# Attention in pairs of units, the first mixture in blocks of 256 tokens, the logits four tiles at a time

## The chip, the core and the metric

The kernel runs on one core of one Trainium2 chip. The metric is device time in microseconds (us) of one launch, the median of three runs. The engines are named as the profile names them: PE (TensorE, matmuls), DVE (VectorE), ACT (ScalarE), POOL (GpSimd) and SP (SyncE, which issues the DMAs). Every engine works off its own list of instructions strictly in the order in which the program wrote them.

## The reference

Three stages follow each other, all in float32. Cut to what matters:

```python
for t in range(S):                                   # attention: (B,H,S,D) = (4,8,768,48)
    cur = einsum('bhd,bhe->bhde', u[None] * kt, vt)
    y[:, :, t] = einsum('bhd,bhde->bhe', rt, state + cur)
    state = wt[..., None] * state + einsum('bhd,bhe->bhde', kt, vt)
x = y as (3072, 384)
x = ((x @ w1) * (x @ w2)) @ w3 @ w_out               # first mixture, 384 -> 1024 -> 384
logits = x @ w_gate                                  # 8 experts, then 8 rounds of row and column norms
out = sum_e P[:, e:e+1] * (relu(x @ w1[e]) @ w2[e])  # second mixture, weighted by the normed P
```

## The kernel before

**Attention.** The 3072 tokens are 24 units of 128 tokens. In a unit the recurrence is written as small matmuls: `sc` (64x64 scores of the keys K and the receptances R), `trn` (four 128x128 transposes of K), `yt1` (scores times values), `up` (the state's increment), `Sn` (the new state, eight short DVE instructions) and `yt2` (R times the old state), 64x64 tiles in the corners of the PE. Before them DVE and POOL prepare a unit: two scans of the decay (`scan_f` L279, `scan_g` L283), `ks` and `rp` (products with k and r, L296 and L300), `kx`, `rx`, `rk` and `ec` on POOL (L306, L312, L274 and L275, L321), `cc` on DVE.

**First mixture.** The tokens go through in eight blocks of 384 (`BLK`). For each of eight slices f of the hidden width there are nine matmuls `pa` and nine `pb` (high and low parts of x and of the weights, two tiles of 128x384 per tag and so at most two `pb` on their way), ACT copies `pa` (`asb`), DVE multiplies it with `pb` (`gs`, L478), ACT and POOL split the product (`gh`, `gl`). Then 72 matmuls `po` with the folded weights give the x of the second mixture. That is 8*18 + 72 = 216 matmuls of 384 columns a block. `moe_log` (L528) forms a block's logits: nine small matmuls `pl`, a DVE copy, one transpose `plt`, a DVE copy.

**Second mixture.** For n = 0 to 63 (four batches of 768 tokens times sixteen pairs of hidden slices) the program runs `zp` matmuls of 256 columns and `yp` matmuls of 384. Sums and differences of x tiles that it needs are made ahead by `pre_x` (sums L699, low parts L706, then a DMA to memory); DVE does this for the first three batches during the attention.

**What sets the order.** Units 0 to 6 come from the hand-written list `START`, which the change leaves alone. From slice `S0 = 28` on, a loop over slices s does in each slice one f of `pa`/`pb`, or one of four parts of `po`, and one phase of unit n = s // 4: phase 1 is [`yt2` of the unit before, `sc`, `trn`], phase 2 is [`yt1`, `up`, `Sn`], and the last unit of a block has its `yt2` in phase 3. The preparation of the next unit waits in the queue `aux`, two entries a slice, and `pre_x` sits at places in a table (`PLACES`, `LASTPLACES`). Every attention input has two buffers (`nat[nm, u_ % 2]`). All matmuls are written by the helper `mm`, L114, so the trace shows one line for them.

Of the kernel before, what the change touches and what calls it, by code (L numbers as in the profile page):

```python
# [61 lines left out]
def tile_rwkv_moe_sinkhorn_moe(  # L62
# [28 lines left out]
    BLK = 384  # L91
    UB = BLK // P
    NB = NT // BLK
# [4 lines left out]
    T = 256  # L98
# [26 lines left out]
    lt = const.tile([GP * UB, P], F32, name="lt")  # L125
# [167 lines left out]
    def ks(n):  # L293
        st[n]["K"] = t = att.tile([P, 34 * 32], F32, tag="K", bufs=1, name="Kt")
        gv = st[n]["G"][:, 1:529].rearrange("p (c b s) -> p b c s", b=2, s=33)[:, :, :, 1:33]
        (nc.gpsimd if n in KS_POOL else nc.vector).tensor_tensor(diag(t), nat["k", n % 2].rearrange("p (a b s) -> p b a s", b=2, s=32), gv, op=ALU.mult)  # L296

    def rp(n):
        st[n]["R"] = t = att.tile([P, 34 * 32], F32, tag="R", bufs=2, name="Rt")
        (nc.gpsimd if n in RP_POOL else nc.vector).tensor_tensor(off(t)[:, ::-1], nat["r", n % 2].rearrange("p (a b s) -> p b a s", b=2, s=32),  # L300
                                tot(n)[:, :, :, 0:32], op=ALU.mult)

    def kx(n):
        t = st[n]["K"]
        for g, m_ in enumerate((st[n]["M"][:, 1, :], tot(n)[:, 1, :, 32])):
            nc.gpsimd.tensor_tensor(off(t)[:, g], diag(t)[:, 1 - g], m_.unsqueeze(2).to_broadcast([P, 8, 32]),  # L306
                                    op=ALU.mult)

    def rx(n):
        t = st[n]["R"]  # L310
        for g, m_ in enumerate((st[n]["M"][:, 0, :], tot(n)[:, 0, :, 32])):
            nc.gpsimd.tensor_tensor(diag(t)[:, g], off(t)[:, 1 - g], m_.unsqueeze(2).to_broadcast([P, 8, 32]),  # L312
                                    op=ALU.mult)
# [11 lines left out]
    def sc(n):  # L325
        Rt, Kt = st[n]["R"], st[n]["K"]
        st[n]["sc"] = s_ = [psa.tile([P, NP, DP], F32, tag=f"sc{h}", name=f"sc{h}") for h in range(2)]
        for p in range(NP):
            for c in range(2):
                for h in range(2):  # L330
                    cs = slice((4 * p + 2 * c) * 32, (4 * p + 2 * c + 2) * 32)
                    mm(s_[h][64 * c:64 * c + 64, p, :], Kt[64 * h:64 * h + 64, cs], Rt[64 * h:64 * h + 64, cs],
                       True, True, pos=(64 * h, 64 * c))

    def trn(n):
        if n - 1 in st:
# [4 lines left out]
        for p in range(NP):  # L341
            mm(pn[:, p, :], st[n]["K"][:, (16 + 4 * p) * 32:(20 + 4 * p) * 32], ident, True, True, tr=True)

    def kn_(n):
        st[n]["kn"] = t = att.tile([P, NP, P], F32, tag="kn", name="kn")
        nc.scalar.activation(t, st[n]["pn"], AF.Copy)
# [8 lines left out]
    def yt1(n):  # L355
        d = st[n]
        A, vt = d["A"], nat["v", n % 2].rearrange("p (h d) -> p h d", d=DP)
        d["yp"] = yp = [psa.tile([P, NP, DP], F32, tag=f"yt{c}", name=f"yt{c}") for c in range(2)]
        for p in range(NP):
            for h in range(2):  # L360
                for c in range(2):
                    rs = slice(64 * c, 64 * c + 64)
                    o = 64 * (h if c else 1 - h)
                    mm(yp[c][o:o + 64, p, :], vt[rs, 2 * p + h, :], A[rs, h, p, :],
                       p == 0, n % UPB == 0 and c == 0 and p == NP - 1, pos=(64 * c, o))

    def up_(n):
        d = st[n]
        vt = nat["v", n % 2].rearrange("p (h d) -> p h d", d=DP)
        d["up"] = up = [psa.tile([P, NP, DP], F32, tag=f"sc{c}", name=f"up{c}") for c in range(2)]  # L370
        for p in range(NP):
            for h in range(2):
                for c in range(2):
                    rs = slice(64 * c, 64 * c + 64)
                    mm(up[c][64 * h:64 * h + 64, p, :], d["kn"][rs, p, 64 * h:64 * h + 64], vt[rs, 2 * p + h, :],
                       True, True, pos=(64 * c, 64 * h))

    def sn_(n):
# [3 lines left out]
        for c in range(2):  # L382
            sn = att.tile([P, NP, DP], F32, tag="S", bufs=3, name="Sn")
# [12 lines left out]
    def yt2(n):  # L396
        yp, ss, Rt = st[n]["yp"], st[n]["ss"], st[n]["R"]
        for p in range(NP):
            for h in range(2):
                for c in (1, 0):  # L400
# [16 lines left out]

    def xd_(n):
        blk, q = n // UB, n % UB
        xt = xr[blk]  # L420
        if blk == NB - 1 or q == UB - 1:
            ts_ = slice(q * P, (q + 1) * P) if blk == NB - 1 else slice(0, BLK)
            for j in range(KD):
                for h in range(2):
                    nc.sync.dma_start(xt[64 * h + D:64 * h + 64, j, ts_],
                                      xt[64 * h + DQ * j:64 * h + DQ * (j + 1), NP - 1, ts_])

    def stage_a0(n):
        rk(n)
        aux.extend([lambda f=f: f(n) for f in (scan_f, scan_g, small, ks, rp, kx, rx)] + [lambda: (cc(n), ec(n))])  # L430

    def each(n, *fs):
        for f in fs:
            f(n)
# [3 lines left out]
    def x_high(blk, q=None):  # L438
        xt = xr[blk]
        if blk not in xs:  # L440
            xhl = moe.tile([P, 2, KD, BLK], F32R, tag="xhl", name="xhl")
            xs[blk] = (xhl[:, 0], xhl[:, 1])
        xh, xl = xs[blk]
        ts_ = slice(0, BLK) if q is None else slice(q * P, (q + 1) * P)
        nc.scalar.activation(xh[:, :, ts_], xt[:, 0:KD, ts_], AF.Copy)

    def x_low(blk, q=None):
        xt = xr[blk]
        xh, xl = xs[blk]
        ts_ = slice(0, BLK) if q is None else slice(q * P, (q + 1) * P)  # L450
        nc.vector.tensor_tensor(xl[:, :, ts_], xt[:, 0:KD, ts_], xh[:, :, ts_].bitcast(F32), op=ALU.subtract)
# [5 lines left out]
    def ab(blk, f, nm, wh, wl):  # L457
        xh, xl = xs[blk]
        m_t[nm, blk, f] = pt = ps.tile([P, BLK], F32, tag={"pa": "mA", "pb": "mB"}[nm], bufs=2, name=nm)
# [47 lines left out]
    def moe_x2(blk, i, parts=X2S):  # L507
        gh, gl = g_t[blk]
        n_ = KD * NF * 3 // parts
        for m in range(i * n_, (i + 1) * n_):  # L510
            q, rest = divmod(m, 3 * NF)
            f, c = divmod(rest, 3)
            if rest == 0:
                if 0 not in x2:
                    x2_open()
                po_t[blk] = ps.tile([P, BLK], F32, tag="mAmB"[2 * (q % 2):][:2], bufs=2, name="po")
# [3 lines left out]
            if rest == 3 * NF - 1:  # L520
                t0, t1 = blk * BLK, (blk + 1) * BLK
                while t0 < t1:
                    dst, o = x2_at(q, t0)
                    n = min(T - o, t1 - t0)
                    nc.scalar.activation(dst[:, o:o + n], po[:, t0 - blk * BLK:t0 - blk * BLK + n], AF.Copy)
                    t0 += n

    def moe_log(blk, step, pool=None, tag="mA", bufs=2):  # L528
        pool = pool or ps
        if step == 0:  # L530
            pl = pool.tile([GP * UB, P], F32, tag=tag, bufs=bufs, name="pl")
# [728 lines left out]
```

## Time and profile before

| | |
|---|---|
| median of 3 runs | 1915.16 us (1914.37 to 1915.44) |
| profiled execution | 1915.92 us, of which the span from the first to the last instruction is 1914.2 us |
| PE busy | 99% of the span |
| DVE, ACT, POOL busy | 72%, 36%, 34% |
| granted clock | 1.00 |

A busy share counts the time in which at least one instruction of the engine is on its way. The attention and the first mixture run together until about 437 us; after that the second mixture alone runs to the end.

### The profile page before, as it was taken

Reading aid. Unit: us, or ns where it says so; the run is one execution under the profiler, and the core shown is the slowest. Engines: PE = TensorE matmul, PEld = TensorE weight load, DVE = VectorE, ACT = ScalarE, POOL = GpSimd, SP = SyncE. Lnnn points to the kernel's source line nnn. Section 1 sums busy time; section 2 is a strip of 40 time slices with the busy share of each in tenths; the row PEclk is TensorE's granted clock in tenths of the full one; section 3 lists DMA queues with packets and bytes.
Section 4 is the critical chain, followed back from the end, with each engine's and each line's share of the span. In section 5 each row is a group of like instructions: output and inputs, shape, how many; then the busy total and the mean of one; then the engine's idle time right before and its main releaser. Section 6 shows DMA issues by size and latency. Waiting matters only on the chain.

```text
span 1914.2 us, 38103 instructions
## 1 busy us (share of the span) xinstructions
PE 1888.8 (99%) x15499; PEld 1842.9 (96%) x15499; DVE 1378.7 (72%) x2409; ACT 686.2 (36%) x1322; POOL 650.0 (34%) x867
## 2 busy tenths in 40 slices
PE   6999999999999999999999999999999999999999
PEld 3799999999999999999999999999999999999999
DVE  8866777765887887676767677667677777667666
ACT  6733333344333333333333333333333333333322
POOL 6766666635431313122222222222323231322200
PEclk9999999999999999999999999999999999999999
DMA  9622444346655555555555555555555555555463
GB/s 379 230 87 91 140 134 140 105 148 239 235 184 191 190 196 197 182 199 183 202 188 197 185 200 187 193 176 208 175 200 185 197 194 193 191 182 188 173 204 121
DMA packets 90494, 353.76 MB, mean 185 GB/s; under 512 B 10384, under 2 KB 34256, under 8 KB 64592
## 3 DMA queue, kind: packets, MB, share of 16 engines
q1 hardware_dynamic: 90320, 351.34, 53.1%
q8 instruction: 122, 2.00, 0.4%
q14 instruction: 52, 0.43, 0.1%
HBM read 329.67 MB, written 20.45 MB: 183 GB/s over the span
## 4 chain that ended last, share of the span: by engine, by line
PE 94%; DMA 2%; DVE 2%; ACT 1%; issue 0%; SPq 0%; DVEq 0%; ACTq 0%
PE yp L114 41%; PE zp L114 34%; PE po L114 5%; PE pa L114 5%; PE pb L114 5%; DMA raw<-in_moe_w_dram 1%; PE yt L114 1%; PE w34ps L114 1%; PE trn L114 1%; DMA nat_kn<-in_kn_dram 1%; PE sc L114 1%; PE up L114 0%; PE pl L114 0%; DVE cvp L229 0%; DVE Sn L388 0%
## 5 line engine op out<-in xcount | busy, mean ns | idle before, releaser
L114 PE MATMUL zp<-xc,w1c 128*128 128x256 f32 x5760 | 793.7, 277 | 1.0 <-DVE ct L915 0.6
L114 PEld LDWEIGHTS zp<-xc,w1c 128*128 128x128 f32 x5760 | 766.7, 188 | 4.8 <-ACT ct L922 1.3
L114 PE MATMUL yp<-w2h,hl 128*128 128x384 f32 x1536 | 515.0, 335 | 0.6 <-DVE hl L912 0.6
L114 PE MATMUL yp<-w2l,hh 128*128 128x384 f32 x1536 | 514.6, 335 | 0.0
L114 PE MATMUL yp<-w2h,hh 128*128 128x384 f32 x1536 | 513.1, 334 | 0.0
L907 ACT ACTIVATE hh<-ct 128x512 fp32r<-128x512 f32 x384 | 236.8, 632 | 526.3 <-DVE ct L915 265.8
L915 DVE TENSOR_TENSOR ct<-ct,zp 128x512 f32<-128x512 f32 x576 | 377.3, 681 | 47.0 <-PE zp L114 41.4
L620 POOL TENSOR_TENSOR w1c<-w1s,w1c 128x512 fp32r<-128x512 f32 (+1 forms) x120 | 127.6, 1064 | 779.9 <-ACT w1c L616 779.9
L922 ACT ACTIVATE ct<-zp 128x512 f32<-128x512 f32 x256 | 153.6, 600 | 440.8 <-PE zp L114 440.8
L114 PEld LDWEIGHTS yp<-w2h,hl 128*128 128x128 f32 x1536 | 288.3, 188 | 1.0 <-DVE hl L912 0.9
L114 PEld LDWEIGHTS yp<-w2h,hh 128*128 128x128 f32 x1536 | 288.4, 188 | 0.2 <-issue 0.2
L114 PEld LDWEIGHTS yp<-w2l,hh 128*128 128x128 f32 x1536 | 288.4, 188 | 0.0
L1087 DVE SCALAR_TENSOR_TENSOR acc<-yp,Pm,acc 128x384 f32<-128x384 f32 x336 | 205.8, 613 | 103.9 <-PE yp L114 103.8
L912 DVE SCALAR_TENSOR_TENSOR hl<-ct,hh 128x512 fp32r<-128x512 f32 x384 | 276.5, 734 | 0.0
L918 DVE TENSOR_TENSOR ct<-ct,zp 128x512 f32<-128x512 f32 x128 | 87.9, 687 | 162.8 <-PE zp L114 162.8
L918 DVE TENSOR_TENSOR ct<-zp,ct 128x512 f32<-128x512 f32 x128 | 88.3, 690 | 74.6 <-ACT ct L922 62.7
L620 POOL TENSOR_TENSOR w1c<-w1raw,w1c 128x128 fp32r<-128x128 f32 (+1 forms) x90 | 56.7, 630 | 195.3 <-ACT w1c L616 195.3
L612 POOL TENSOR_TENSOR w1s<-w1raw 128x128 f32<-128x128 f32 x240 | 120.8, 524 | 0.2
L487 POOL TENSOR_TENSOR gl<-gs,gh 128x384 fp32r<-128x384 f32 x64 | 75.4, 1179 | 104.0 <-ACT gh L483 101.2
L114 PE MATMUL pa<-xhl,w1h 128*128 128x384 f32 x384 | 100.4, 342 | 1.5 <-ACT w34s L255 1.5
L114 PE MATMUL pb<-xhl,w2h 128*128 128x384 f32 x384 | 98.1, 336 | 0.4 <-DVE cv L230 0.4
L478 DVE TENSOR_TENSOR gs<-pb,asb 128x384 f32<-128x384 f32 x64 | 35.4, 553 | 66.6 <-PE pb L114 48.1
(130 smaller groups left out, 1908.6 us busy)
## 6 DMA issues: line engine op xcount, KB each, us to landing
xc<-xd SPq DMA_DIRECT2D x192, 1024.0 KB, 4.9
xc<-xd SPq DMA_DIRECT2D x64, 768.0 KB, 4.3
xd<-x2s SPq DMA_DIRECT2D x53, 256.0 KB, 2.7
w1raw<-in_e_w_dram SPq DMA_DIRECT2D x32, 384.0 KB, 3.1
w2raw<-in_e_w_dram SPq DMA_DIRECT2D x32, 384.0 KB, 3.1
raw<-in_moe_w_dram SPq DMA_DIRECT2D x8, 1024.0 KB, 9.5
nat_w<-in_w_dram SPq DMA_DIRECT2D x24, 264.5 KB, 3.4
nat_k<-in_kt_dram SPq DMA_DIRECT2D x24, 256.0 KB, 4.0
```

Source lines behind the costliest of these rows:

```text
L114: nc.tensor.matmul(o, lhsT, rhs, start=start, stop=stop, **kw)
L478: nc.vector.tensor_tensor(t, m_t.pop(("pb", blk, f)), m_t.pop(("asb", blk, f)), op=ALU.mult)
L487: nc.gpsimd.tensor_tensor(gl[:, f, :], m_t.pop(("gs", blk, f)), gh[:, f, :].bitcast(F32), op=ALU.subtract)
L612: eng.tensor_tensor(tmp_[:, many.index(r), :], at_(a), at_(b), op=ALU.add if sg == 1 else ALU.subtract)
L620: eng.tensor_tensor(lo[:, d0:d1, :], sv, hi[:, d0:d1, :].bitcast(F32), op=ALU.subtract)
L907: nc.scalar.activation(hh, src, AF.Relu)
L912: nc.vector.scalar_tensor_tensor(hl, src, 0.0, hh.bitcast(F32), op0=ALU.max, op1=ALU.subtract)
L915: nc.vector.tensor_tensor(o, a, b_, op=ALU.add)
L918: nc.vector.tensor_tensor(o, a, b_, op=ALU.subtract)
L922: nc.scalar.activation(t, src, AF.Copy)
L1087: nc.vector.scalar_tensor_tensor(dst, yp, so["Pm"][:, tt, e:e + 1], dst, op0=ALU.mult, op1=ALU.add)
```

## The change

Units 0 to 6 stay as they are. The blocks of the first mixture are now 384, 384 and then nine of 256 tokens. From unit 7 on (unit 7 by itself, then 8 and 9, 10 and 11, up to 22 and 23) a block of 256 tokens goes with a pair of units, in a cycle c of 24 steps: eight steps of nine `po` matmuls, then sixteen that are alternately a `pa` and a `pb`. At the start of a cycle stands `turn`: `yt2` of both old units, `sc` of both new ones, `trn` of both. After step 8 stands `middle`: `yt1` of both, `up` of both, then `Sn` of both. The preparation of the two units of the next cycle (`prep`) is placed by steps.

K and R are now pairs of half tiles, so `ks` and `rp` are two DVE instructions each; they take over the second input buffers, and from unit 10 on the inputs r, k, w, rn and kn have one buffer each. The logits are formed in groups of four tiles of 128 tokens, six groups instead of eight blocks. All of the third batch's `pre_x` now comes before the second mixture starts, and three of the eight first weight preparations of the second mixture (`sp_w1`) go to POOL.

```diff
-    BLK = 384
+    T = 256
+    BLKS = [(0, 384), (384, 384)] + [(t, T) for t in range(768, NT, T)]
+    FU = 6
+    NC = NB - 2
+    def src(nm, u_):
+        return nat[nm, u_ % 2 if u_ < ONE or nm == "v" else 0]
...
-    def sc(n):
-        st[n]["sc"] = s_ = [psa.tile([P, NP, DP], F32, tag=f"sc{h}", name=f"sc{h}") for h in range(2)]
+    def pair(nm):
+        return [psa.tile([P, 2, NP, DP], F32, tag=f"{nm}{c}", name=f"{nm}{c}") for c in range(2)]
+
+    def sc(*us):
+        s_ = pair("sc")
...
-    def moe_log(blk, step, pool=None, tag="mA", bufs=2):
+    UL = P // GP
+    def moe_log(grp, step, pool=None, tag="mA", bufs=2):
...
+    def turn(k_old, k_new):
+        old, new = (units(k) if 0 <= k <= NC - 1 else () for k in (k_old, k_new))
+        for n in old:
+            yt2(n)
+        if new:
+            front(*new)
+        if old:
+            xraw(*old)
+            xd_(old[-1])
+        if new:
+            front_end(*new)
...
+    for k in range(NC):
+        step(k, -0.5, lambda k=k: turn(k, k + 1))
+        step(k, 4.6, lambda k=k: x_high(k + 2))
+        step(k, 5.6, lambda k=k: x_low(k + 2))
+        if k + 1 < NC:
+            step(k, 9 - 0.5, lambda k=k: middle(*units(k + 1)))
+        if k + 2 < NC:
+            n = FU + 2 * k + 4
+            prep(n, 24 * k + 1)
+            prep(n + 1, 24 * k + 12)
...
+            if sb_ < NS - 2:
+                t_, w_, d_ = 24 * 3 * sb_ + 9.7 + 4.2 * m_, WORK[m_ % 4], (5, 9)
...
+    for c in range(-1, NC):
+        for j in range(10 if c < 0 else 0, 24):
+            run(24 * c + j)
+            if j < 8:
+                moe_x2(c + 1, j, 8)
+            else:
+                f = (j - 8) // 2
+                if j % 2 == 0:
+                    pa(c + 2, f)
+                    asb(c + 2, f)
+                else:
+                    pb(c + 2, f)
+                    gs(c + 2, f)
```

What this does to the order, first on PE, at the place where unit 9 ends and unit 10 begins. Before (of the rows of `yt` and of `sc`, which alternate between two tiles, the first two stand):

```order
L114 MATMUL pb<-xhl,w2h 128x384 x2
L114 MATMUL pb<-xhl,w2l 128x384
L114 MATMUL yt_2479<-Rt,Sn 64x64
L114 MATMUL yt_2478<-Rt,Sn 64x64
...
L114 MATMUL sc_2648<-Rt,Kt 64x64
L114 MATMUL sc_2649<-Rt,Kt 64x64
...
L114 MATMUL trn<-ident,Kt 128x128 x4
L114 MATMUL pa<-xhl,w1h 128x384 x2
```

One unit's `yt2`, `sc` and `trn` stand between two runs of wide matmuls. The same place of PE in the changed kernel, where units 8 and 9 end and 10 and 11 begin (`nat_n`, `nat_k`, `nat_w`, `kn` and `s_more` are buffers that now hold halves of K and R, and states):

```order
L113 MATMUL pb<-xhl,w2l 128x256
L113 MATMUL yt_2193<-Rt,nat_n_109 64x64
...
L113 MATMUL yt_2193<-nat_k_102,Sn 64x64
...
L113 MATMUL sc_2567<-Rt,Kt 64x64
...
L113 MATMUL sc_2567<-Rt,nat_w_106 64x64
...
L113 MATMUL trn<-ident,nat_n_109 128x128 x4
L113 MATMUL trn<-ident,kn 128x128 x4
L113 MATMUL po<-gh,w34h 128x256
```

Two units' small matmuls now stand in one group. Next DVE, from the new state of a unit to the next unit's scans, before:

```order
L388 SCALAR_TENSOR_TENSOR Sn<-Sn,T_2454,up_2730 128x64 x4
L388 SCALAR_TENSOR_TENSOR Sn<-Sn,T_2454,up_2731 128x64 x4
L300 TENSOR_TENSOR Rt<-nat_r_99,Ft 128x2x8x32
L478 TENSOR_TENSOR gs<-pb,asb 128x384
L706 TENSOR_TENSOR x2s<-x2s 128x256 x3
L699 TENSOR_TENSOR x2s<-x2s 128x256 x2
L317 TENSOR_REDUCE cc<-rk 128x8
L279 SCALAR_TENSOR_TENSOR Ft<-nat_w_106,d_63 128x528
```

In the changed kernel, the same stretch of DVE in the third cycle (c = 2), from the second half of the new states on:

```order
L452 SCALAR_TENSOR_TENSOR s_more<-nat_n_109,T_2952,sc_3351 128x64 x4
L762 TENSOR_TENSOR x2s<-x2s 128x256
L532 TENSOR_TENSOR gs<-pb,asb 128x256
L359 TENSOR_REDUCE cc<-rk 128x8
L532 TENSOR_TENSOR gs<-pb,asb 128x256
L755 TENSOR_TENSOR x2s<-x2s 128x256 x2
L298 SCALAR_TENSOR_TENSOR Ft<-nat_w_105,d_63 128x528
L762 TENSOR_TENSOR x2s<-x2s 128x256
L532 TENSOR_TENSOR gs<-pb,asb 128x256
L302 SCALAR_TENSOR_TENSOR Gt<-nat_w_105,d_63 128x527
L309 RECIPROCAL Mt<-Ft 128x16
L310 TENSOR_TENSOR T_3500<-Ft 128x8
```

The `gs` instructions stand between the scans and the sums of `pre_x`, behind sixteen `Sn` instead of eight.

## Rows read from the trace of the kernel before

**Rows 1.** Profile page, part 1: busy time and share of the span, instructions.

```profile
PE 1888.8 (99%) x15499; PEld 1842.9 (96%) x15499; DVE 1378.7 (72%) x2409; ACT 686.2 (36%) x1322; POOL 650.0 (34%) x867
```

**Rows 2.** Windows: stretch, length, busy time of each engine, granted clock, DMA share, GB/s.

```profile
182.89:230.60 47.71, 47.71 (x634) 45.34 (x629) 34.87 (x74) 18.28 (x44) 31.88 (x30) 1.00 0.45 136
400.00:500.00 100.00, 98.44 (x663) 96.06 (x662) 66.85 (x134) 42.81 (x94) 38.21 (x47) 1.00 0.68 238
```

**Rows 3.** Timeline, TensorE, 150 to 169 us: start, length, instructions with equal ones merged.

```profile
150.00 0.34 PE L114 MATMUL pb<-xhl,w2l 128*128 128x384 f32 x1
150.27 0.69 PE L114 MATMUL yt<-Rt,Sn 64*64 64x64 f32 x32
150.79 0.65 PE L114 MATMUL sc<-Rt,Kt 64*64 64x64 f32 x32
151.37 0.66 PE L114 MATMUL trn<-ident,Kt 128*128 128x128 f32 x4
151.78 0.59 PE L114 MATMUL pa<-xhl,w1h 128*128 128x384 f32 x2
152.21 0.34 PE L114 MATMUL pa<-xhl,w1l 128*128 128x384 f32 x1
...
154.82 0.34 PE L114 MATMUL pb<-xhl,w2l 128*128 128x384 f32 x1
155.09 0.69 PE L114 MATMUL yt<-ec,nat_v 64*64 64x64 f32 x32
155.60 0.65 PE L114 MATMUL up<-nat_v,kn 64*64 64x64 f32 x32
...
156.64 0.33 PE L114 MATMUL pa<-xhl,w1l 128*128 128x384 f32 x1
...
159.24 0.34 PE L114 MATMUL pb<-xhl,w2l 128*128 128x384 f32 x1
...
160.59 0.33 PE L114 MATMUL po<-gh,w34l 128*128 128x384 f32 x1
...
166.31 0.34 PE L114 MATMUL po<-gh,w34l 128*128 128x384 f32 x1
...
167.21 0.65 PE L114 MATMUL trn<-ident,Kt 128*128 128x128 f32 x4
...
168.05 0.34 PE L114 MATMUL po<-gh,w34l 128*128 128x384 f32 x1
```

**Rows 4.** Timeline, TensorE, the logits of one block.

```profile
181.59 0.86 PE L114 MATMUL pl<-x2s,gate 128*32 128x128 f32 x18
182.37 0.69 PE L114 MATMUL yt<-Rt,Sn 64*64 64x64 f32 x32
```

**Rows 5.** Timeline, TensorE, matmuls of 256 columns, two places.

```profile
456.07 2.28 PE L114 MATMUL zp<-xc,w1c 128*128 128x256 f32 x18
...
474.48 1.53 PE L114 MATMUL zp<-xc,w1c 128*128 128x256 f32 x12
475.85 0.33 PE L114 MATMUL yp<-w2h,hh 128*128 128x384 f32 x1
```

**Rows 6.** Timeline, VectorE, four instructions between 120 and 215 us.

```profile
120.13 1.25 DVE L279 TENSOR_TENSOR_SCAN Ft<-nat_w,d 128x528 f32<-128x528 f32 x1
...
204.03 1.61 DVE L388 SCALAR_TENSOR_TENSOR Sn<-Sn,T,up 128x64 f32<-128x64 f32 x8
...
207.38 0.56 DVE L478 TENSOR_TENSOR gs<-pb,asb 128x384 f32<-128x384 f32 x1 [1.14 <-PE pb L114]
...
212.56 2.09 DVE L279 TENSOR_TENSOR_SCAN Ft<-nat_w,d 128x528 f32<-128x528 f32 x1 [1.23 <-POOL Rt L312]
```

**Rows 7.** Timeline, GpSimd, around 120 us.

```profile
125.32 0.62 POOL L306 TENSOR_TENSOR Kt<-Kt,Mt 128x256 f32<-128x256 f32 x1 [8.67 <-DVE T L291]
```

**Rows 8.** Groups by line, VectorE, 130 to 430 us: count, busy, mean ns, idle before.

```profile
L699 DVE TENSOR_TENSOR x2s<-x2s 128x256 f32<-128x256 f32 x34 | 24.8, 732 | 0.4
```

More of the change, by code (lines that the diff above doesn't have):

```diff
@@ new lines, in ks @@
+        if n < FU + 3:
+            t = att.tile([P, 34 * 32], F32, tag="K", bufs=1, name="Kt")
+            st[n]["K"] = both(t)
+            eng.tensor_tensor(diag(t), kv, gv, op=ALU.mult)
+            if n == FU + 2:
+                ka_home.extend([both(t)[0], nat["w", 1][:, 0:HALF]])
+                kk_ring.extend([st[n - 1]["kn"].rearrange("p a b -> p (a b)"), both(t)[1], nat_n1[:, 0:HALF]])
+                kk_ring.rotate(-2)
+        else:
+            st[n]["K"] = K = ka_home[n % 2], kk_next()
+            for g in range(2):
+                eng.tensor_tensor(alt(K[g], g), kv[:, g], gv[:, g], op=ALU.mult)
@@ new lines, in rp @@
+    def rp(n):
+        eng = nc.gpsimd if n in RP_POOL else nc.vector
+        rv = src("r", n).rearrange("p (a b s) -> p b a s", b=2, s=32)
+        tv = tot(n)[:, :, :, 0:32]
+        if n < FU + 3:
+            t = att.tile([P, 34 * 32], F32, tag="R", bufs=2, name="Rt")
+            st[n]["R"] = both(t)
+            eng.tensor_tensor(off(t)[:, ::-1], rv, tv, op=ALU.mult)
+            if n == FU + 2:
+                ra_home.extend([st[n]["R"][0], st[n - 1]["R"][0]])
+                rb_home.extend([st[n]["R"][1], nat["k", 1], nat["r", 1], st[n - 1]["R"][1]])
+        else:
+            st[n]["R"] = R = ra_home[n % 2], rb_home[(n - FU - 2) % 4]
+            for g in range(2):
+                eng.tensor_tensor(alt(R[1 - g], g), rv[:, g], tv[:, g], op=ALU.mult)
@@ L353, in tile_rwkv_moe_sinkhorn_moe @@
     state = {}
[L355 to L376, printed above, removed]
+    def yt1(*us):
+        yp = pair("yt")
+        for u_, n in enumerate(us):
+            st[n]["yp"], st[n]["yu"] = yp, u_
+            A, vt = st[n]["A"], src("v", n).rearrange("p (h d) -> p h d", d=DP)
+            for p in range(NP):
+                for h in range(2):
+                    for c in range(2):
+                        rs = slice(64 * c, 64 * c + 64)
+                        o = 64 * (h if c else 1 - h)
+                        mm(yp[c][o:o + 64, u_, p, :], vt[rs, 2 * p + h, :], A[rs, h, p, :], u_ == 0 and p == 0,
+                           n <= FU and n % UPB == 0 and c == 0 and p == NP - 1, pos=(64 * c, o), skip=n > FU)
@@ new lines, in up_ @@
+    def up_(*us):
+        up = pair("sc")
+        for u_, n in enumerate(us):
+            vt = src("v", n).rearrange("p (h d) -> p h d", d=DP)
+            st[n]["up"] = [t[:, u_] for t in up]
+            for p in range(NP):
+                for h in range(2):
+                    for c in range(2):
+                        rs = slice(64 * c, 64 * c + 64)
+                        mm(up[c][64 * h:64 * h + 64, u_, p, :], st[n]["kn"][rs, p, 64 * h:64 * h + 64],
+                           vt[rs, 2 * p + h, :], True, True, pos=(64 * c, 64 * h))
@@ L382, in sn_ @@
         for c in range(2):
[L383 removed]
+            sn = s_new(n)
             if s0 is None:
@@ L423, in xd_ @@
+    def xd_(n):
+        blk, q = UBLK[n]
+        xt = xr[blk]
+        if (q + 1) * P == BLKS[blk][1]:
             for j in range(KD):
                 for h in range(2):
[L425 to L434, printed above, removed]
@@ L436, in tile_rwkv_moe_sinkhorn_moe @@
-    xs = {}
[L438 to L442, printed above, removed]
-        xh, xl = xs[blk]
[L444 to L451, printed above, removed]
+                    nc.sync.dma_start(xt[64 * h + D:64 * h + 64, j, :],
+                                      xt[64 * h + DQ * j:64 * h + DQ * (j + 1), NP - 1, :])
@@ new lines, in prep, with put @@
+    def prep(n, base, scale=1.0):
+        def put(d, *fs):
+            event(base + 0.5 + d * scale, *fs)
+        put(0, lambda: rk(n), lambda: scan_f(n))
+        put(1, lambda: scan_g(n))
+        put(2, lambda: small(n))
+        put(3, lambda: ks(n))
+        put(4, lambda: rp(n))
+        put(5, lambda: kx(n))
+        put(6, lambda: rx(n))
+        put(8.8, lambda: cc(n))
+        put(9.6, lambda: ec(n))
+        for nm, d in (("rn", 2), ("kn", 2), ("w", 4), ("k", 6), ("r", 7)):
+            m = n + (2 if n < ONE - 1 else 1)
+            if m < NU and not n == ONE - 1 - 0:
+                put(d, lambda nm=nm, m=m: load(m, (nm,)))
@@ L787, in tile_rwkv_moe_sinkhorn_moe, with front, front_end, middle @@
+    def front(*us):
+        sc(*us)
+        for n in us:
+            trn(n)
+    def front_end(*us):
+        for n in us:
+            kn_(n)
+        for n in us:
+            cp_(n)
+    def middle(*us):
+        yt1(*us)
+        up_(*us)
+        for n in us:
+            sn_(n)
     tx0 = []
@@ new lines, in tile_rwkv_moe_sinkhorn_moe, with units @@
+    s_more = att.tile([P, NP, DP], F32, name="s_more")
+    def units(k):
+        return tuple(u_ for u_ in (FU + 2 * k, FU + 2 * k + 1) if u_ > FU)
+    def turn(k_old, k_new):
[9 more added lines that the diff above has]
+            front_end(*new)
+    step(-1, 10 - 0.5, lambda: turn(-1, 0))
@@ new lines, in tile_rwkv_moe_sinkhorn_moe @@
+    step(-1, 13 - 0.5, lambda: middle(*units(0)), lambda: load(FU + 3, ("v",)))
+    prep(FU + 2, -24 + 10, 0.6)
+    prep(FU + 3, -24 + 16.5, 0.6)
+    for k in range(NC):
[8 more added lines that the diff above has]
+            prep(n + 1, 24 * k + 12)
+            step(k, 11.6, lambda n=n: load(n, ("v",)), lambda n=n: load(n + 1, ("v",)))
@@ new lines, in open_w @@
+    def open_w():
+        st_attn.close()
+        pools["w"] = ctx.enter_context(tc.tile_pool(name="wp", bufs=1, side="right", reuse_waits="tile"))
+        ld_w1(0)
+        ld_w1(1)
+        st_pa.close()
+        pools["z"] = ctx.enter_context(tc.tile_pool(name="psz", bufs=1, space=PSUM, side="right",
+                                                    reuse_waits="tile"))
+        for g in range(2):
+            spaced(pools["w"], [P, 4, T], F32, f"w1c{g}0", "unused")
+            ld_x(0, g)
@@ L1143, in sk_both @@
         sk_rows()
-    for x_ in late:
-        sk.append(lambda x_=x_: moe_log(*x_, pool=pools["y"], tag="col", bufs=1))
+    for t_ in range(2):
+        sk.append(lambda t_=t_: moe_log(NTT // UL - 1, t_, pool=pools["y"], tag="col", bufs=1))
     sk.extend([sk_max0, sk_max1, sk_max2])
```

315 lines of the change are left out of this document (135 added, 180 removed).

## The prediction

> **What bounds the kernel now.** I read the page first: PE is busy 99% of the span, DVE 72% [rows 1]. Then the windows. Three units and one block of 384 tokens take 47.71 us, and PE is busy in all of it; DVE is busy 34.87 us of it, POOL 31.88, ACT 18.28, at a granted clock of 1.00, the 2.4 GHz level [rows 2]. Only the handover to the second mixture shows PE idle, 1.56 us between 400 and 500 us [rows 2]. So in the changed stretch nothing is waited for, and time can be won only by giving PE less to do; whatever newly makes PE wait is lost in full. The profiled execution took 1915.92 us, 0.76 above the median shown; I sum against it and take the 0.76 off at the end.
>
> **What PE does there, priced.** The timeline gives starts. Wide matmuls of 384 columns follow each other every 0.1733 us: from the third of the `po` at 160.59 to the 36th at 166.31 are 33 intervals, 5.72 us [rows 3]. A group of small matmuls costs the time from the last wide start before it to the third after it, less three such intervals (0.52):
> - `yt2`, `sc`, `trn`: 152.21 - 150.00 - 0.52 = 1.69 us
> - `yt1`, `up`: 156.64 - 154.82 - 0.52 = 1.30
> - `yt2` alone: 160.59 - 159.24 - 0.52 = 0.83
> - `sc`, `trn`: 168.05 - 166.31 - 0.52 = 1.22 [all rows 3].
>
> Inside a group `yt2` takes 0.52 until the next starts, `sc` 0.58, `trn` 0.41, `yt1` 0.51 [rows 3]. The rest, 0.18 to 0.31 per group, is getting in and out.
>
> **Term 1, the groups.** Before, the loop has 17 units (7 to 23): eleven groups of the first kind, six of `sc`, `trn`, seventeen of `yt1`, `up`, six `yt2` alone: 11*1.69 + 6*1.22 + 17*1.30 + 6*0.83 = 53.0 us. After: unit 7 keeps 1.22 and 1.30. A full `turn` is 1.69 plus a second `yt2` (0.52), a second `sc` and a second `trn` (0.41). A second `sc` or `up` between other small matmuls has no row; bounds are the 0.58 of one that ends in `trn` and, the other way, the same 32 matmuls with the change of kind off, 0.45. I take `yt1`'s 0.51, the nearest. So 3.13, seven times; the first `turn` has one `yt2`, 2.61; the last two `yt2` alone, 1.35; eight full `middle` 1.30 + 2*0.51 = 2.32 each. Sum 46.95. **Saved 6.0 us** (4.9 to 7.0).
>
> **Term 2, the logits.** `pl` of 18 recorded matmuls takes 0.78 us until the next [rows 4]. In the loop it comes seven times before, five times with four tiles after. By the row four tiles lie between the same time and a third more (1.04): 5.5 against 3.9 to 5.2. **Saved 0.8** (0.3 to 1.6). The last group is late in both.
>
> **Term 3, the wide matmuls.** Blocks of 256 do the same columns in 1944 matmuls instead of 1296 (9 blocks of 216, for 6). No `pa`, `pb` or `po` of 256 columns was run before; the nearest are the `zp`. Twelve from 474.48 to 475.85 come every 0.1142 us; eighteen in 2.28 us at 456.07, when PE had just come out of the attention, every 0.118 (the last one takes 0.274, as in the twelve: 1.53 - 11*0.1142) [rows 5]. Two thirds of 0.1733 is 0.1156. So the same columns cost 1944*(0.1142 - 0.1156) = -2.7 us by the one row, and +4.7 by the other. The 384-column intervals of this stretch are even from the third after a group on, which is more like the first row; the small groups break the stream, which is more like the second. I take **0**, and both ends for the range.
>
> The Trainium skill ("TensorE: Matmul & The Clock Gate", "Back-to-back issue gap") puts a fixed 2.5 ns on each matmul over its columns at 2.4 GHz; 648 more matmuls would cost 1.6 us by it, as an estimate. The rows disagree: over 106.7 and 160 ns of columns they show 7 to 11 ns at 256 and 13 at 384, an excess that shrinks with the matmul.
>
> **Term 4, new waits.** A pair of units with its block takes PE 216*0.1156 + 3.13 + 2.32 + about 0.5 for logits = 30.9 us, 15.5 a unit instead of 15.9. Into it must go two thirds of DVE's 34.87, 23.2, and more instructions for the same elements (2.7 more `gs`, four more halves of `ks` and `rp`; some 1 us by `gs`' 0.56 [rows 6], less what is per element): 24.3 of 30.9, 79% where it was 73%. POOL: 21.3 and 2.7 more `gl`, some 22, 71%. On average both fit. The question is the order. `pb` of f+2 needs the tile of `pb` of f, which `gs` frees: three runs of nine lie between, 27*0.1156 = 3.1 us now, 4.7 before. `gs` of the first slices stands behind sixteen `Sn`, twice eight at 1.61 us [rows 6]. From the first `Sn` (after `up` of the first unit, 14.3 us into the cycle) to its end are 16.6 us, and in the cycles c = 2 and 5 DVE has there: `Sn` 3.2, eight `gs` at 0.45 (two thirds of 0.56 to all of it) 3.6, two scans at about 2.0 (2.09 [rows 6]) 4.0, six sums at 0.73 [rows 8] 4.4, the halves of `ks` and `rp`, three lows and two `cc` some 4.5 by the same row: 19.7. The excess, 3.1, is just the lead that PE leaves. Queued behind a late `gs` on DVE are `rp`, and behind that `kx` and `rx` on POOL, for which the next `turn` waits, and `x_low`, which the first `pa` of the next slice needs: walked through in the order of the instructions, `x_low` ends about 0.6 us before PE wants it. In the other cycles there are two sums or fewer, and 1 to 3 us are spare. DMA: inputs with one buffer are loaded again as soon as they are read, some 7 steps before use, and SP's queue holds those loads, the `x` moves and the stores of `pre_x` in this order; I cost it at nothing as long as that lead holds, and up to one load a cycle late if not. At the handover the idle 1.56 us may go or double. I take **+2.0** in all; bounds: 1 us below nothing (the handover), and 10 above, if half the cycles lose 1 to 2.5.
>
> **Sum.** 1915.92 - 6.0 - 0.8 + 0 + 2.0 = 1911.1, less 0.76: **1910.4 us**.
>
> **Rivals.**
> 1. *The 256-column matmuls run at 0.118 all through.* For it: the run nearest in time, and every group interrupts the stream. Against it: most `zp` later come at 0.1142. Gives -6.8 + 4.7 + 2.0, 0.1 less than before: 1915.1, no change that can be told.
> 2. *All fits and the matmuls run at 0.1142.* For it: no PE wait in this stretch before, with DVE at 73%. Gives -6.8 - 2.7 + 0: 1905.7.
> 3. *DVE becomes the bound.* In three units it is idle 12.84 us [rows 2], 4.3 a unit, and the rows show what for: `gs` after 1.14 us for `pb`, a scan after 1.23 us for POOL [rows 6]. If that idle time is not room but part of the chain, a pair takes 24.3 + 8.6 = 32.9 us, 2.0 more than PE needs, and eight pairs lose 16: 1915.9 - 6.8 + 16 - 0.8 = 1924.3. It decides from two thirds of this on (10.6 us lost is slower by 0.2%). For it: the lead of 3.1 us, and a scan of 1.25 us while POOL stood idle for 8.67 us takes 2.09 with POOL at work [rows 6, 7], so squeezing both together stretches both. Against it: `gs` came at once after the wait, and ended long before it was needed.
>
> The Trainium skill ("SBUF — State Buffer", "Who interferes with whom") has the rule behind the last: a DVE instruction with two SBUF inputs and a POOL one that reads SBUF share a port, and one blocks. The trace agrees, 1.25 against 2.09. By it the third rival gets likelier as the cycle gets shorter.
>
> **How the numbers follow.** The forecast has 0.48, rivals 1, 2, 3 have 0.19, 0.20 and 0.13. About 0.2% (3.8 us) is what a measurement of this kernel can tell from no change. The forecast's own range is 1907 to 1915; three quarters of it lie below 1911.3, so faster 0.36 + 0.20 = 0.56; same 0.12 + 0.19 = 0.31; slower 0.13. The range for 8 in 10, 1904 to 1919, takes in rivals 1 and 2 and the first part of the third.
>
> **What would show it.** Right: `turn` at 3.1 and `middle` at 2.3 us in PE's timeline, wide intervals between 0.114 and 0.118 with no lasting change at the groups, PE idle only in c = 2 and 5, named as waiting for `gs` or `x_low`, a cycle of 30 to 31 us. Wrong: idle PE in every cycle, released by DVE or POOL; `sc` waiting for `rx`; `pa` waiting for `x_low` or for the DMA of `x`; scans waiting for loads; a second mixture that starts late.

## The result, and the profile after

The changed kernel takes 1936.15 us (median; 1933.37 to 1936.59) beside 1915.12 us for the kernel before on the same chip: a ratio of 1.0107 with an interval of 1.0091 to 1.0123, 1.1% slower. The forecast was 1910.4 us, with a range up to 1919. The profiled span went from 1914.2 to 1934.8 us.

First the page's busy times [rows 1], then two windows, with columns as in [rows 2]: the handover, and the seven cycles from the first `po` of one block to the first `po` of the seventh after it.

```profile
PE 1892.5 (98%) x16145; PEld 1853.1 (96%) x16145; DVE 1399.9 (72%) x2452; ACT 684.3 (35%) x1342; POOL 651.2 (34%) x903
...
400.00:500.00 100.00, 94.48 (x954) 92.16 (x953) 55.85 (x128) 43.29 (x108) 42.26 (x58) 1.00 0.52 184
...
195.86:432.54 236.68, 225.27 (x3360) 218.43 (x3358) 184.50 (x399) 84.99 (x216) 128.68 (x140) 0.99 0.40 118
```

Where PE was never idle it now is idle for 11.4 of 236.7 us, and a cycle takes a seventh of that stretch, 33.8 us, where 30.9 was forecast. Between 400 and 500 us PE is idle for 5.5 us instead of 1.6. PE's waits behind the start-up name who ends them (the matmul that waited, then the engine and instruction that released it: us in total, times, longest):

```profile
PE plt L113 <- DVE lt L594: 7.0, 5, 2.0
PE pb L113 <- DVE gs L532: 3.8, 5, 1.2
PE yp L113 <- DVE hl L988: 2.4, 1, 2.4
PE pa L113 <- DVE xhl L505: 1.2, 4, 0.3
PE zp L113 <- ACT ct L998: 1.1, 1, 1.1
```

The largest is one that the prediction doesn't have: the logits' transpose `plt`, which reads `lt`, DVE's copy of the logits `pl`. The same place on PE and on DVE (timelines; start, length, in brackets the idle time just before and who ended it):

```profile
209.62 0.28 PE L113 MATMUL pb<-xhl,w2l 128*128 128x256 f32 x1
211.40 0.30 PE L113 MATMUL plt<-ident,lt 128*128 128x128 f32 x1 [1.51 <-DVE lt L594]
...
207.90 0.86 DVE L452 SCALAR_TENSOR_TENSOR Sn<-Sn,T,sc 128x64 f32<-128x64 f32 x4 [1.95 <-PE sc L113]
208.67 0.85 DVE L452 SCALAR_TENSOR_TENSOR nat_n<-Sn,T,sc 128x64 f32<-128x64 f32 x4
209.44 0.85 DVE L452 SCALAR_TENSOR_TENSOR s_more<-nat_n,T,sc 128x64 f32<-128x64 f32 x4
210.21 0.85 DVE L452 SCALAR_TENSOR_TENSOR Sn<-s_more,T,sc 128x64 f32<-128x64 f32 x4
210.97 0.28 DVE L594 COPY lt<-pl 128x128 f32<-128x128 f32 x1
```

`pl` and `middle` end together, so DVE gets the sixteen `Sn` first and the copy `lt` behind them; PE has nine `pb` to do (1.1 us) and then stands before `plt`. DVE was not short of time here: it had been idle for 1.95 us before the first `Sn`.

One of these waits did more. At 346.90, after 1.99 us of idle time, the granted clock was 0.52 for the next 3.4 us, the 1.2 GHz level, and matmuls of 256 columns came every 0.213 us until it was back. After none of the 1.5 us waits did it fall. (Columns as in [rows 2].)

```profile
344.60:346.90 2.30, 0.33 (x3) 0.14 (x2) 2.30 (x12) 0.00 (x0) 0.00 (x0) 1.00 0.01 4
346.90:350.30 3.40, 3.39 (x17) 3.40 (x18) 0.85 (x3) 0.80 (x2) 0.73 (x1) 0.52 0.70 206
350.40:353.00 2.60, 2.60 (x24) 2.60 (x23) 1.98 (x4) 1.11 (x3) 1.06 (x2) 0.99 0.09 32
```

The groups and the wide matmuls on PE (answering to [rows 3, 5]): a `turn`, and a long run of `pa` and `pb`.

```profile
226.77 0.28 PE L113 MATMUL pb<-xhl,w2l 128*128 128x256 f32 x1
226.98 0.69 PE L113 MATMUL yt<-nat_r,Sn 64*64 64x64 f32 x32
...
227.96 0.65 PE L113 MATMUL sc<-Rt,Kt 64*64 64x64 f32 x32
228.43 0.65 PE L113 MATMUL sc<-Rt,nat_w 64*64 64x64 f32 x32
229.00 0.66 PE L113 MATMUL trn<-ident,kn 128*128 128x128 f32 x4
229.50 0.60 PE L113 MATMUL trn<-ident,Kt 128*128 128x128 f32 x4
...
230.17 0.28 PE L113 MATMUL po<-gh,w34l 128*128 128x256 f32 x1
...
213.93 0.28 PE L113 MATMUL pa<-xhl,w1l 128*128 128x256 f32 x1
...
222.57 0.28 PE L113 MATMUL pa<-xhl,w1l 128*128 128x256 f32 x1
```

The `turn` costs 230.17 - 226.77 less three intervals of 0.12, 3.04 us (forecast 3.13). From 213.93 to 222.57 are 72 intervals: 0.1200 us each, not 0.1156, in all nine blocks.

So the 20.0 us from the first `po` to PE's last matmul (1795.8 to 1815.8 us) come out as follows; each interval from one start on PE to the next, less its idle time, is put to its kind:

| | before | after | difference |
|---|---|---|---|
| PE idle | 1.6 | 17.3 | +15.7 |
| wide matmuls at their steady interval (1584 of 384; then 288 of 384 and 1944 of 256) | 274.8 | 282.9 | +8.1 |
| slow wide matmuls outside the groups (after waits, at the lower clock) | 1.1 | 5.9 | +4.8 |
| groups, by the prediction's measure | 60.1 | 51.9 | -8.2 |
| second mixture | 1456.8 | 1456.4 | -0.4 |

### The profile page after: what moved, and what is told of

Read it like the earlier page. It is cut to its first block, busy times and chain, and to the rows that moved or that the text cites. A ratio compares the mean times of both kernels' runs of the same rounds, so it can differ in the third digit from the quotient of the medians.

```text
span 1934.8 us, 39531 instructions
## 1 busy us (share of the span) xinstructions
PE 1892.5 (98%) x16145; PEld 1853.1 (96%) x16145; DVE 1399.9 (72%) x2452; ACT 684.3 (35%) x1342; POOL 651.2 (34%) x903
## 4 chain that ended last, share of the span: by engine, by line
PE 74%; DMA 1%; DVE 1%; POOL 0%; ACT 0%; issue 0%; SPq 0%; DVEq 0%; ACTq 0%
PE yp L113 41%; PE zp L113 33%; DMA w2raw<-in_e_w_dram 0%; DMA xd<-x2s 0%; POOL x2s L755 0%; DVE hl L988 0%; DVE ct L991 0%; DVE acc L1159 0%; ACT hh L983 0%; POOL w1c L676 0%; ACT ct L998 0%; POOL x2s L762 0%; POOL gl L541 0%; PE pcs L113 0%; DVE w2l L736 0%
## 5 line engine op out<-in xcount | busy, mean ns | idle before, releaser
L541 POOL TENSOR_TENSOR gl<-gs,gh 128x256 fp32r<-128x256 f32 (+1 forms) x88 | 76.3, 871 | 127.8 <-ACT gh L537 125.1
L113 PE MATMUL pb<-xhl,w2h 128*128 128x256 f32 (+1 forms) x528 | 108.3, 298 | 4.2 <-DVE gs L532 3.8
L113 PE MATMUL pa<-xhl,w1h 128*128 128x256 f32 (+1 forms) x528 | 107.9, 296 | 2.0 <-DVE xhl L505 1.2
L113 PEld LDWEIGHTS pb<-xhl,w2h 128*128 128x128 f32 x528 | 84.6, 192 | 7.6 <-DVE gs L532 5.5
```

The source lines that it names most:

```text
L113: nc.tensor.matmul(o, lhsT, rhs, start=start, stop=stop, **kw)
L541: nc.gpsimd.tensor_tensor(gl[:, f, :], m_t.pop(("gs", blk, f)), gh[:, f, :].bitcast(F32), op=ALU.subtract)
```

## The experiments

Two causes were to be told apart and priced: DVE's order (or, as a rival, DVE's sum of work), and the 256-column matmuls' 0.12 us. Kernel n is the kernel of experiment n. The chips of these runs were others, on which the kernel before took 1921.7 to 1924.4 us, so everything is compared by its ratio to the kernel before; the changed kernel stands at 1.0107. Each ratio has an error of about 0.001 to 0.0017 either way, so two kernels are told apart by it from some 0.002 (4 us) on. The kernel before has a trace from the first chip alone.

**1. Addresses.** In the changed kernel the weights and the moving data of all `pa`, `pb` and `po` start at equal addresses modulo 256 bytes, by the program's allocations; for `zp` the two are 192 bytes apart.

```diff
+    OFFS = (0, 0, 0, 16, 32, 48, 8, 48, 48, 48, 48)      # words, by block
-        xhl = moe.tile([P, 2, KD, BLKS[blk][1]], F32R, tag="xhl", name="xhl")
+        xhl = moe.tile([P, 2 * KD * BLKS[0][1]], F32R, tag="xhl", name="xhl")[:, o:o + 2 * KD * w_]
...
         (gh and gl likewise, o = OFFS[blk])
```

> The changed kernel with nothing changed but the place of three tiles inside their buffers: in the blocks of 256 tokens the inputs xhl, gh and gl start 0, 64, 128, 192 or 32 bytes further on (blocks 3, 4, 5, 6 by 64, 128, 192, 32 bytes; blocks 7 to 10 by 192; block 2 by 0). In the kernel as it stands weights and moving data of all these matmuls start at equal addresses modulo 256, in the experts' zp they are 192 bytes apart. Theory A (the equal addresses make a 256-column matmul of the mixture take 120 ns where zp takes 114): the shifted blocks run at 114 to 116 ns, block 2 stays at 120, the time falls by 8 blocks x 216 x 5 ns = about 8.6 us, to 1927 or 1928 us. Rival (a fixed 13 ns beside the columns, in this stretch, whatever the addresses): every block at 120 ns, the time stays at 1936 us, within 2.

Ratio 1.0097 (1.0082 to 1.0112). Two blocks' `po`, block 2 at equal addresses and block 3 at 64 bytes:

```profile
194.36 0.28 PE L113 MATMUL po<-gh,w34l 128*128 128x256 f32 x1
...
202.63 0.28 PE L113 MATMUL po<-gh,w34l 128*128 128x256 f32 x1
...
228.24 0.28 PE L113 MATMUL po<-gh,w34l 128*128 128x256 f32 x1
...
236.06 0.28 PE L113 MATMUL po<-gh,w34l 128*128 128x256 f32 x1
```

69 intervals each: 0.1199 and 0.1133 us. With 128 bytes `po` stayed at 0.1200 (`pa` 0.1185); with 64 or 192 bytes a stretch ran at about 0.1134 or 0.1178, with 32 at 0.117. Theory A holds for the matmuls (some 6 us less in all); but PE's idle time grew by 2.5 us, and the fall of the ratio, 0.0010, lies within the error.

**2. `plt` three groups later.**

```diff
-        step(2 * g_ - 1, 9.6, lambda g_=g_: moe_log(g_, 1))
+        step(2 * g_ - 1, 15.6, lambda g_=g_: moe_log(g_, 1))
...
```

> The changed kernel with the transpose of the logits (plt) placed three pa/pb groups later in its cycle, so that the copy lt that it waits for has 6 us more. Theory A (the five waits of plt for DVE's lt, 7.0 us together, are lost because the copy stands behind sixteen Sn on DVE and nothing else on PE is due for them): they go, with the slow matmuls after each, and the time falls by 7 to 9 us, to 1927 to 1929 us. Rival (DVE is behind as a whole after the sixteen Sn, the wait only passes to the next pb's gs): PE's waits for gs grow by what plt's lose, time 1934 to 1936 us.

Ratio 1.0083 (1.0066 to 1.0100): half of theory A. `plt` waits no more, but its tile shares two buffers with `pa`, and the next `pa` now waits for DVE's copy `L` out of it:

```profile
PE pa L113 <- DVE L L598: 4.2, 4, 1.5
PE pb L113 <- DVE gs L532: 2.6, 4, 1.2
```

**3. `Sn` in two runs.**

```diff
         up_(*us)
-        for n in us:
-            sn_(n)
+        sn_(us[0])
...
+            step(k, 13.5, lambda k=k: sn_(units(k + 1)[1]))
```

> The changed kernel with the Sn of the second unit of a pair issued five steps later (behind pb and gs of the third group), so that DVE has eight Sn in one run instead of sixteen; plt stays where it is. Theory A (DVE's unbroken run of sixteen Sn, 3.2 us, is what holds lt and gs back): plt's waits fall from 7.0 us to under 2, gs's from 3.8 to about 2, time 1928 to 1931 us. Rival (DVE's sum of work in these stretches is the bound, its order isn't): the waits pass to gs of the fourth and fifth group, time 1934 to 1938 us.

Ratio 1.0068 (1.0053 to 1.0083), the lower end of theory A: `plt`'s waits fell from 7.0 to 0.4 us, `gs`' only to 3.4, so those have another cause. `lt` now stands behind eight `Sn`:

```profile
PE pb L113 <- DVE gs L532: 3.4, 5, 0.9
...
PE plt L113 <- DVE lt L594: 0.4, 1, 0.4
...
206.62 0.85 DVE L452 SCALAR_TENSOR_TENSOR nat_n<-Sn,T,sc 128x64 f32<-128x64 f32 x4
207.39 0.28 DVE L594 COPY lt<-pl 128x128 f32<-128x128 f32 x1
```

**4. Combinations of x2 off DVE.** This kernel leaves out the sums for the first two batches and lets ACT copy their low parts, so its output is another.

```diff
-            for m, (sg, _) in enumerate(ts[1:], 1):
+            for m, (sg, _) in enumerate(ts[1:] if sb == NS - 2 else (), 1):
...
+            if sb < NS - 2:
+                nc.scalar.activation(hr[:, 1, :], sv, AF.Copy)     # low part, on ACT
```

> The changed kernel with DVE freed of the combinations of x2 for the first two sequences (their sums are left out, so the output is another; their low parts are a copy on ACT). Theory A (the waits of pb for gs in the third and sixth cycle, 3.8 us, and of pa for xhl, 1.2 us, come from the combinations that DVE does between Sn and gs): both go, plt's 7.0 us stay since only Sn stands ahead of lt: time 1930 to 1932 us. Rival (the waits come from the scans and K, R products of the pair alone): gs waits stay at 3 us or more, time 1935 to 1937 us.

Ratio 1.0061 (1.0046 to 1.0076), more than theory A asked: `gs`' and `xhl`'s waits are gone, `plt`'s stay, and the slow matmuls (5.9 us in the table) fell to 2.8.

```profile
PE plt L113 <- DVE lt L594: 7.3, 5, 1.5
...
PE pb L113 <- DVE gs L532: 0.5, 2, 0.4
```

**5. The same combinations placed elsewhere**, none left out.

```diff
-                t_, w_, d_ = 24 * 3 * sb_ + 9.7 + 4.2 * m_, WORK[m_ % 4], (5, 9)
+                t_ = 24 * (3 * sb_ + m_ // 5) + 14.7 + 2.5 * (m_ % 5) + 0.5 * (m_ % 5 == 4)
+                w_, d_ = WORK[m_ % 4], (3, 6)
```

> The changed kernel with only the combinations of x2 placed outside the steps 8 to 14; the work on every engine stays the same, unlike in the run that left them out. Theory A (their place on DVE is what holds gs and xhl back): pb's waits for gs fall from 3.8 to under 1.5 us, pa's for xhl from 1.2 to 0.5 or less, plt's stay at 7 us; ratio to the kernel before 1.0070 to 1.0090. Rival (DVE's sum of work): gs waits 3 us or more, ratio 1.0100 to 1.0115.

Ratio 1.0072 (1.0057 to 1.0087), theory A: `gs`' waits fell to 0.9 us with the same work on DVE, busy for 183.9 us in the seven cycles (184.5 in the changed kernel). `xhl`'s did not (1.5 us).

```profile
194.72:426.58 231.86, 223.32 (x3359) 216.73 (x3358) 183.88 (x399) 84.95 (x215) 129.72 (x140) 1.00 0.40 122
```

**6. Edits 1 (192 bytes in all nine blocks) and 3 together.**

> The changed kernel with xhl, gh and gl 192 bytes further on in all nine blocks of 256 tokens, and the second unit's Sn five steps later: the two edits that lowered the time by themselves, together. Theory A (two costs that add up: equal addresses, and sixteen Sn in one run): against the kernel before the ratio falls from 1.0107 of the changed kernel by 0.0039 (the split) and by 1944 x 4 to 6 ns (0.004 to 0.006), to 1.001 to 1.003. Rival (once the matmuls are faster PE waits longer for DVE, as PE's idle time grew by 2.5 us with the shifted addresses): only the split's part stays, 1.005 to 1.007.

Ratio 1.0044 (1.0029 to 1.0059), between the two: the matmuls fell to 0.1164 us on average, and `gs`' waits rose to 5.5 us, `xhl`'s to 2.5. A faster PE meets the same DVE earlier.

**7. Edits 1, 3 and 5 together.**

> The kernel of the two edits (addresses, Sn in two runs) with a third: the combinations of x2 for the first two sequences are placed outside the steps 8 to 14, so that none stands on DVE between Sn and gs. Theory A (without them pb's waits for gs fell from 3.8 to 0.5 us, and the slow matmuls after waits from 7.4 to 3.5 us; their place is what counts, not their sum): a further 4 to 8 us, ratio to the kernel before 0.997 to 0.999. Rival (DVE's sum of work in the third and sixth cycle counts, so that the waits move elsewhere): no further gain, ratio 1.001 to 1.003.

Ratio 1.0030 (1.0019 to 1.0040): theory A's size was missed, and the rival's range has the value; the gain of 0.0014 on kernel 6 lies within the error. `gs`' waits fell to 1.8 us, but `x_low` now stood behind the combinations, and `xhl`'s rose from 2.5 to 4.0.

```profile
PE pa L113 <- DVE xhl L508: 4.0, 6, 1.1
...
PE pb L113 <- DVE gs L535: 1.8, 4, 0.6
```

**8. And `x_high`, `x_low` two steps earlier.**

```diff
-        step(k, 5.6, lambda k=k: x_low(k + 2))
+        step(k, 3.6, lambda k=k: x_low(k + 2))               (x_high 4.6 -> 2.6)
```

> The kernel of the three edits (addresses, Sn in two runs, combinations outside steps 8 to 14) with the split of the next block's input (x_high, x_low) two steps earlier in each cycle, ahead of the combinations on DVE. Theory A (in the kernel of three edits pa waits for xhl six times, 4.0 us, because x_low now stands behind the combinations): these waits go, with some 1 to 2 us of slow matmuls after them: ratio to the kernel before 0.9995 to 1.0010. Rival (DVE's sum of work, the wait passes to gs or to the turn's trn): 1.0025 to 1.0040.

Ratio 1.0006 (0.9997 to 1.0016), theory A: the wait for `xhl` fell to 0.2 us, and the second mixture begins at 437.5 us (437.2 before, 458.9 in the changed kernel). This is as fast as the kernel before, as far as can be told, and not faster.

**9. Kernel 8 with the addresses back.**

> The changed kernel with its three edits of place on DVE (Sn in two runs, combinations outside steps 8 to 14, x_low two steps earlier) and with xhl, gh and gl back at equal addresses. Theory A (the two costs of the change add up: waits behind DVE and the addresses): the 256-column matmuls return to 120 ns, 1944 x 4.0 ns = 7.8 us more than with the shift (115.8 ns), PE's idle time stays near 7 us: ratio to the kernel before 1.0035 to 1.0050, against 1.0006 with the shift and 1.0107 for the changed kernel. Rival (the places alone give it all, the shift only feeds waits, as the first run with shifted addresses moved the time by 2 us): 1.0005 to 1.0020.

Ratio 1.0031 (1.0019 to 1.0044), just under theory A's range: the matmuls are back at 0.1200 us, and PE's idle time fell to 4.9 us in all, since a slower PE meets DVE later. The same seven cycles, here and in kernel 8:

```profile
193.00:416.25 223.25, 222.03 (x3359) 216.62 (x3358) 174.01 (x399) 85.59 (x215) 123.95 (x140) 1.00 0.42 127
...
192.16:411.43 219.27, 216.73 (x3359) 210.92 (x3357) 173.94 (x398) 85.33 (x216) 124.02 (x140) 1.00 0.42 129
```

PE is idle for 1.2 us instead of 11.4, with the same 399 instructions on DVE. They also got shorter: DVE is busy for 174.0 us instead of 184.5, and of the 10.5 us the 24 scans gave 6.2 (39.4 to 33.2) and the seven `x_low` 2.1 (8.8 to 6.7). For `gs` experiment 5 shows the order alone, at 183.9 us; for the whole of kernel 9 the order and the shorter instructions are not told apart. The places on DVE are worth 1.0107 - 1.0031, some 14.6 us, and the addresses 1.0031 - 1.0006, some 4.8.

**10. Two more of the experts' preparations on POOL, on kernel 8.**

```diff
...
-    nc.gpsimd if m_ in (3, 6, 7) else nc.vector
+    nc.gpsimd if m_ in (1, 3, 5, 6, 7) else nc.vector
...
```

> The kernel of the four edits with two more of the eight preparations of the experts' first weights done by POOL in the last cycle, where POOL is busy 12 of 45 us. Theory A (the wait of 2.1 us for hl and those for ct at the experts' start are DVE's backlog from the last cycle): they fall by 1 to 2 us, ratio 0.0005 to 0.001 under that of the kernel of four edits. Rival (they come from the transfers and buffers of the new stage): no difference.

Ratio 1.0031 (1.0019 to 1.0043): neither, it is slower. `hl` was waited for 1.7 us instead of 2.2 and `ct`'s 1.1 went, but ACT now stood waiting for POOL's slower sums, with `asb` queued behind, and `pa` waited 2.1 us for that. The clock then fell to the 1.2 GHz level for 3.4 us, and the 256-column matmuls ran at 0.1168 instead of 0.1158 us, 1.9 us more, at the same addresses. (Its profiled run also reached the loop 3.5 us later, where nothing was changed.)

```profile
441.52 0.52 ACT L677 ACTIVATE w1c<-tx 128x384 fp32r<-128x384 f32 x1 [2.42 <-POOL tx L673]
441.95 0.36 ACT L531 ACTIVATE asb<-pa 128x256 f32<-128x256 f32 x1
```

**11. Kernel 10 with 64 bytes instead of 192** (`OFFS` of 16).

> The kernel just described with xhl, gh and gl 64 bytes further on instead of 192. Theory A (with any shift that isn't 0 or 128 bytes the 256-column matmuls run at 113.5 or 117.8 ns, and which of the two a stretch takes is not set by the shift): time within 3 us of the other, both values seen. Rival (64 bytes is the better relation: the one block with it ran po at 113.3): po at 113.3 to 113.6 in all nine blocks, 2 to 3 us less.

Ratio 1.0023 (1.0014 to 1.0032), not told apart from kernel 10. `po` ran at 0.1178 us in seven of nine blocks, so 64 bytes is not the better relation, and the shift doesn't choose between 0.1134 and 0.1178.

**12. Addresses alone, in the kernel before.**

```diff
-    d1 = const.tile([P, 16 * 33 + 1], BF16, name="d1")
     w34l = moe.tile([P, NF, DM], F32R, name="w34l")
+    d1 = moe.tile([P, 16 * 33 + 1], BF16, name="d1")
```

> The kernel before, with the constant d1 placed behind w34l instead of ahead of it, which changes addresses alone: po's weights and moving data go from equal addresses modulo 256 to 64 bytes apart (576 matmuls of 384 columns), zp's third weight slot from 192 bytes apart to equal (1800 of 256 columns), yp's first two slots from 192 to equal (of 384 columns), while pa and pb stay equal. Theory A (equal addresses cost a matmul of 256 columns 4 to 6 ns, whatever the stage, and one of 384 columns nothing, since yp takes 173 ns at 192 bytes and po 173 at 0): zp with the third slot slows from 114 to 118 to 120 ns, po and yp stay at 173, time 7 to 11 us longer (ratio 1.004 to 1.006). Rival B (the addresses count at any size): po falls to 167 ns, which gives back 3.8 us, yp's first slots rise. Rival C (the addresses matter only in the first mixture): nothing changes, ratio 1.000 within 0.0015.

Ratio 1.0140 (1.0125 to 1.0156): more than any theory had. `po` of 384 columns stayed at 0.1734 us, against rival B. `zp` slowed by 3.4 ns on average, in all three weight slots, not only in the one whose relation became equal (0.1182 there, 0.1167 to 0.1179 in the others, 0.1142 before), and `yp` by 3.0 ns. Some 0.5 ns of `zp`'s and 0.4 of `yp`'s is the chip: kernels 5 to 7 ran on this one, with `zp` at the addresses of the kernel before, and took 0.5 ns more for `zp` and 0.4 for `yp` than the first chip's trace. `zp` before and here (behind the busy time stands the mean duration of one in ns, whose end is modelled):

```profile
L114 PE MATMUL zp<-xc,w1c 128*128 128x256 f32 x5532 | 761.6, 277 | 0.0
...
L114 PE MATMUL zp<-xc,w1c 128*128 128x256 f32 x5417 | 765.5, 281 | 0.2 <-DVE ct L918 0.2
```

So the place of data costs in the second mixture too, but "weights and moving data equal modulo 256" is not the whole rule.

## Why the prediction was wrong

- **Terms 1 and 2** (groups -6.0, logits -0.8) were right in kind and somewhat small: -8.2 us by the same measure, -7.8 for the groups, beyond the 7.0 that Term 1 allowed, and -0.4 for the logits, with the slow start of `plt` after its waits in it. `turn` took 3.04 and `middle` 2.21 us, against 3.13 and 2.32, and the `yt2` of unit 6, which the sum left out, no longer stands alone. `pl` of four tiles took what the recorded one took.
- **Term 3** (wide matmuls, taken at 0, at most +4.7) measured +8.6 by its own formula, 1944 x 0.0044 us (+8.1 in the table). The failed step is the inference "an excess that shrinks with the matmul". It set `zp` of 256 columns beside `pa` of 384 and put the difference down to the size; the two also lie differently in memory. At equal addresses the excess over the columns is 13.3 ns at 256 as at 384, a fixed price per matmul, and 648 more of them cost 8.6 us. With other addresses (kernel 8) the mean is 0.1158, the 0.1156 of the forecast. The Trainium skill ("SBUF — State Buffer", "Who interferes with whom") gives the moving data and the weights a read port each, independent of one another; by that a shift of one against the other changes nothing, and experiments 1 and 9 disagree.
- **Term 4** (new waits, taken at +2.0, at most +10) measured +15.7 of idle time and 4.8 of slow matmuls. The places that it named were right, and their price too small: `gs` 3.8 us (2.8 of it in the third and sixth cycle, the rest in two others), `x_low` 1.2, the handover 4.4 instead of 1.6. DVE's work was 26.4 us a pair (184.5 / 7) and not 24.3. The trace names no DMA as what ended a wait of PE here, as forecast. The step that failed is its walk along DVE's queue: it asked what of the `gs` stands behind the sixteen `Sn`, and not what else does. `lt` does, PE needs it nine matmuls later, and that gave 7.0 us of waits, and one of them the fall of the clock.
- **Rival 3** (DVE becomes the bound) came nearest in time, 1924.3. As a bound by DVE's sum of work it was wrong: experiment 5 has the same work on DVE in another order, and `gs`' waits are nearly gone; experiment 3 has the same instructions with eight `Sn` moved, and `plt`'s are. It was the order, as Term 4 said. That squeezing stretches the scans, which the rival also said, is so in the traces (39.4 us for 24 scans in the changed kernel, 33.2 in kernel 9); how much time that cost is not shown. Rival 1 (0.118 throughout) was the right kind, still too low.
- What is left of the forecast gain: kernel 8 has the groups' gain (8.1 us by the table's measure) and the forecast interval, and loses 5.7 us to idle time (7.3 instead of 1.6), half of it at the handover, and some 3 to slow matmuls (4 instead of 1.1). That is why it ends at 1.0006 and not at 0.9975. How to mend the handover stays open; experiment 10 was no way.

## What to carry to other kernels

When small steps of two units are put together on one engine's queue, list everything that comes to stand behind the longer run, small copies first, and compare the run with what the waiting engine still has to do: here 3.4 us of DVE work stood against 1.1 us of PE work. Don't carry an interval from one matmul to another before their operands' addresses have been compared as well as their sizes. What is won on an engine whose feeders barely keep up arrives only in part: the shifted addresses made the matmuls faster by some 6 us in experiment 1 and by 8 us from kernel 9 to kernel 8, and PE's idle time took back 2.5 and 2.4 us of that.

## What the runs showed of the hardware

- In the first mixture, matmuls of 256 columns with a weight load each ran steadily at one of three intervals: 0.1134, 0.1178 and 0.1200 us. Weights and moving data 0 bytes apart modulo 256 gave the last, 128 nearly so; 64 or 192 gave one of the first two, which could change from stretch to stretch. At 384 columns `po` took 0.1734 us at 0 and at 64 bytes.
- `zp` at unchanged addresses took 0.1140 us on average on the chip of the result, 0.1146 on the chip of experiments 5 to 7 and 0.1153 on three others. Over 5760 of them the 1.3 ns are 7.5 us; the kernel before took 8.7 to 9.3 us longer on these three.
- Moving one constant, which shifted what lies behind it by 64 bytes, cost the kernel before 1.4% on one and the same chip. Which pair of addresses decides is open.
- Ten times in the traces of this loop and of the handover PE was idle for 1.98 to 2.39 us. Five of them were followed by 3.4 us at the 1.2 GHz level (the next thirty matmuls took 1.2 to 1.6 us longer than thirty like them at full clock), five were not; of the idle times up to 1.76 us none was.
